# Group 0 of a recurrent-attention output moved inside SBUF, and its rows kept in a new order

## The chip, the core and the metric

One core of a Trainium2 chip runs the whole program. Its engines work side by side, each with its own queue of instructions: PE (TensorE, matrix products), DVE (VectorE), ACT (ScalarE), POOL (GpSimd) and SP (SyncE, which here only issues transfers). Sixteen DMA engines move data between DRAM and SBUF, and within SBUF. SBUF is the core's memory of 128 partitions; products land in PSUM, which has eight banks here called "bank". The metric is the device time of one execution in microseconds; less is better.

## The reference

Inputs q, k, v, alpha are (4, 8, 768, 48): batch, heads, sequence, head width. Weights w1, w2 are 384 x 1024, w3 is 1024 x 1024, w_out is 1024 x 384.

```python
for t in range(S):
    state = alpha[:, :, t, :, None] * state + np.einsum('bhd,bhe->bhde', k[:, :, t], v[:, :, t])
    y[:, :, t] = np.einsum('bhd,bhde->bhe', q[:, :, t], state)
x = y.transpose(0, 2, 1, 3).reshape(B * S, H * D)
a = x @ w1
b = x @ w2
return (a * b @ w3) @ w_out
```

So x has 3072 tokens of 384 values: head h fills the values 48 h to 48 h + 47.

## The kernel before

**Tiling.** The sequence is cut into 24 chunks of 128 tokens (`n`), 6 for each batch. Three chunks make a group (`g`, 384 tokens), so there are 8 groups. Two heads share the 128 partitions as a pair: head 2j in partitions 0 to 47, head 2j+1 in 64 to 111 (DP = 64); partitions 48 to 63 and 112 to 127 hold padding. There are four pairs (NP = 4).

**Attention.** The loop `for n in range(N + 1)` overlaps steps of neighbouring chunks. `load_a` and `load_kq` fetch alpha, k and q; `logs` and `decays` build decays with a logarithm, a product with a triangular matrix and two exponentials (L324, L343, L349, L350); `decayed(n + 2)` multiplies k and q with them on DVE (L359); `transposed` turns them with PE (L381) and ACT copies them out (L383); `scores` multiplies k and q (L454, later L430) and DVE masks the result (L457, later L440); `attend_state` and `attend` form the output y transposed, 48 or 64 rows of a head by 128 tokens, in two banks (L474, L485, later L482). Here the halves of the partitions mean something else: the lower half (0 to 63) carries heads 0 to 3, the upper half heads 4 to 7, 48 rows each and 16 rows of padding, and `y[i]` block `j` holds head 2j + i of each half.

**Output of attention.** ACT copies the two banks into a tile x (L489), `later` takes two transfers for it, and `store()` hands them to SP: 48 rows of each half go to the DRAM tile xd of the group (L305), whose rows are in the order of the reference, value 48 h + d.

**Gates.** `load_x(g)` brings xd[g] back as xT, 128 partitions by 3 blocks (`kk`) of 384 tokens: value kk x 128 + p (L501). For group 0 this stands at the end of chunk 4; for groups 1 to 4 at the top of chunks 8, 11, 15, 19, on SP; later visits to groups load on POOL. xT has one buffer. `split_x` cuts xT into three parts of fewer bits (L507, L508, L509), and for group 0 runs in chunk 6 (FIRST). `gate` multiplies them with w1 and w2, likewise in three parts (L515, 9 products in a run of three parts by three `kk`), and stores the product of both (L590).

**Weights.** w1 and w2 come as 64-bit floats and are turned into 32-bit floats by `to_fp32` (DMA L236; ACT L244, L249; DVE L245, L248, L251, L252, L253), and cut in three by `load_gates` (L260, L262, and L265 or two PE products L276, L277). A call handles 128 rows (one `kk`) by 512 columns (a `half`) of one weight: 12 calls, 6 for each half. Up to three are fetched ahead; half 0 is done in chunk 5, half 1 afterwards. `to_fp32` already takes several sources for w3 and w_out, each into its rows of the tile.

**Order.** The text's order, priorities of a planner, and `after_marks` (an instruction goes behind a named one on its engine) fix each engine's order. Waits are put in for every pair of accesses that touch the same bytes.

**After attention** the remaining gates run (`todo`, `visits`), w3 and w_out are multiplied into one matrix, and `project` forms the output.

Of the kernel before, what the change touches and what calls it, by code (L numbers as in the profile page):

```python
# [10 lines left out]
FP32 = mybir.dt.float32  # L11
# [37 lines left out]
def kernel(  # L49
# [12 lines left out]
    nc = tc.nc  # L62
    B, H, S, D = q.shape
    C = 128
# [5 lines left out]
    DP = 64  # L70
# [8 lines left out]
    LATE = 10  # L79
    PAIRED = 8  # L80
    TURNED = 8
    assert D <= DP and DM % C == 0 and DF % CW == 0 and S % C == 0 and N % G == 0
    assert DM <= 512 and TG <= 512

# [138 lines left out]
    for x in Ts + decs:  # L223
        nc.gpsimd.memset(x, 0.0)

    def to_fp32(*srcs, width=None):

        n = width or sum(src.shape[1] for src in srcs)
        raw = rawp.tile([C, n], I64, tag="raw", name="raw")
        for i, src in enumerate(srcs):  # L230
            if width:
                rows = ds(i * src.shape[0], src.shape[0])
                to = raw[rows] if len(src.shape) == 2 else raw[rows].rearrange("p (b c) -> p b c", b=src.shape[1])
            else:
                to = raw[:, ds(i * src.shape[1], src.shape[1])]
            nc.sync.dma_start(out=to, in_=src)  # L236
        yield
        words = raw.bitcast(U32).rearrange("p (n w) -> p n w", w=2)
        low, high = words[:, :, 0], words[:, :, 1]

        mant = cvt.tile([C, n], FP32, tag="mant", name="mant")
        top = mant.bitcast(U32)
        rest = cvt.tile([C, n], FP32, tag="rest", name="rest", bufs=2)
        nc.scalar.activation(rest, low, AF.Copy, scale=2.0 ** -52)  # L244
        nc.vector.tensor_scalar(top, high, 0x000FFFFF, 0x00100000, op0=ALU.bitwise_and, op1=ALU.bitwise_or)  # L245

        power = cvt.tile([C, n], U32, tag="power", name="power", bufs=2)
        nc.vector.tensor_scalar(power, high, 20, 0x7FF, op0=ALU.logical_shift_right, op1=ALU.bitwise_and)  # L248
        nc.scalar.activation(power, power, AF.Relu, scale=2.0 ** 23, bias=rebias)  # L249
        yield  # L250
        nc.vector.scalar_tensor_tensor(mant, top, 2.0 ** -20, rest, op0=ALU.mult, op1=ALU.add)  # L251
        nc.vector.scalar_tensor_tensor(power, high, 0x80000000, power, op0=ALU.bitwise_and, op1=ALU.bitwise_or)  # L252
        nc.vector.tensor_mul(mant, mant, power.bitcast(FP32))  # L253
        yield
        return mant

    def load_gates(i, kk, half):
        w = yield from to_fp32((moe_w1, moe_w2)[i][ds(kk * C, C), ds(half * CW, CW)])
        h, l, m = (w12[half][:, x, i, kk, :] for x in range(3))
        nc.scalar.activation(h, w, AF.Copy, scale=(1.0 - 2.0 ** -13) / P)  # L260
        yield
        mark["l"] = nc.vector.scalar_tensor_tensor(l, h.bitcast(FP32), -P, w, op0=ALU.mult, op1=ALU.add).ins  # L262
        done.append((i, kk, half))
        if half:
            nc.vector.scalar_tensor_tensor(m, h.bitcast(FP32), P + 1.0, w, op0=ALU.mult, op1=ALU.subtract)  # L265
        else:
            thirds.append((m, h, l))
# [33 lines left out]
    def store():  # L301

        while later:
            dst, src = later.popleft()
            nc.sync.dma_start(out=dst, in_=src)  # L305
# [171 lines left out]
    def attend(n):  # L477
        (y, heads), ms, vc = st.pop(("y", n)), st.pop(("ms", n)), st.pop(("v", n))
        for j, i, to in heads:
            if turned(n):  # L480
                w = vts[n % 2][:, j, :] if i else vc[:, 2 * j, :]
                nc.tensor.matmul(to[:, DP:], w, ms[:, i, j, DP:], start=False,  # L482
                                 stop=(j % HP == HP - 1), skip_group_check=True)
            else:
                nc.tensor.matmul(to, vc[:, 2 * j + i, :], ms[:, i, j, :], start=(n % NCH == 0 and j % HP == 0),  # L485
                                 stop=(j % HP == HP - 1), skip_group_check=True)
        x = work.tile([C, HP, 2, C], FP32, tag="x", name="x", bufs=4)
        for i in range(2):
            copied = nc.scalar.copy(x[:, :, i], y[i])  # L489
        ends_of_part1[1] = copied.ins  # L490
        x = x.rearrange("p j i t -> p (j i) t")

        g, c = divmod(n, G)
        to = xd[g].rearrange("(b h d) t -> b d h t", b=2, d=D)
        for half in range(2):
            later.append((to[half, :, :, ds(c * C, C)], x[ds(DP * half, D)]))


    def load_x(g, queue=nc.sync):
        st["xT", g] = xp.tile([C, KM, TG], FP32, tag="xT", name="xT")  # L500
        queue.dma_start(out=st["xT", g], in_=xd[g].rearrange("(k p) t -> p k t", p=C))  # L501

    def split_x(g, i):
        x = st.pop(("xT", g))
# [184 lines left out]
    for n in range(N + 1):  # L689
        if not 1 < n < FIRST:  # L690
            store()
        if n in loads:
            load_x(loads[n])
        if n != 1 and not 2 < n <= FIRST:
            load_a(n + 5)
        raws = (3, 3, 3, 3, 2, 2, 3, 3)[n] if n < 8 else 4
        for m in (n + 3,) * (n <= FIRST) + (n + 4,) * (n >= FIRST):
            load_kq(m)
            if 2 < n <= FIRST and m == n + 3:
                load_a(n + 5)  # L700
            if 1 < n < FIRST:
                store()
            if n < FIRST - 2:
                fetch(raws)
        if n >= FIRST:
            load_v(n + 2)
        if n:
            attend_state(n - 1)
        if n < N:
            scores(n)  # L710
        else:
            for j in range(NP):
                for i in range(2):
                    attend_low(n - 1, j % 2, i, i ^ (j < 2))
        transposed(n + 1)
        if n == 1:
            decays(3)
            load_a(6)
            with after_marks(("e", 3)):
                logs(4)  # L720
        if n == FIRST + 1:
            run(2)
        if n < FIRST:
            with after_marks("pool"):
                load_v(n + 2)
        if n - 2 in begin and n > FIRST:
            g, tiles = begin[n - 2]
            with after_marks(("ms", n), ("qkT", n + 1)):
                split_x(g, 0)
            fill.extend(gate(g, f) for f in tiles)  # L730
        if n == FIRST:
            with after_marks("l", ("qkT", n + 1)):
                split_x(0, 0)
            fill.extend(gate(0, f) for f in begin[n - 3][1])
        pieces = ((3, 3, 2, 0) if n > FIRST + 3 else (0, 3, 3, 0))[(n - FIRST) % 4] if n >= FIRST else 0
        if n == 0:
            with after_marks(("qkT", 0)):
                logs(2)
            decays(2)
            with after_marks(("e", 2)):  # L740
                logs(3)
        early, ready = n < FIRST, len(thirds) if n > 2 else n // 2
        marks = (*[("qkT", n + 1)] * (n < N - 1), *[("qk", n + 1), ("ms", n)] * early, *["x3"] * (n - 2 in begin and n > FIRST))
        if n < N - 2 and n != FIRST:
            with after_marks(*marks):
                convert(2 if early else 1, raws)
        advance(n)
        turn_v(n)
        if n:
            attend(n - 1)  # L750
        outer(n)
        if n > FIRST:
            third(ready)
        run(pieces > 0)
        if early:
            with after_marks(*marks):
                convert(1, raws)
        with after_marks(*[("ms", n)] * (n < 3)):
            decayed(n + 2)
        if not early:  # L760
            with after_marks(*[("qkT", n + 1)] * (n < N - 4)):
                logs(n + 4)
        if n == 4:
            load_x(0)
        convert(early and n > 0, raws)
        run(pieces > 1)
        if n:
            decays(n + 3)
        if n <= FIRST:
            third(ready)  # L770
        if 0 < n < FIRST:
            with after_marks(("e", n + 3)):
                logs(n + 4)
        if n == FIRST:
            with after_marks("x3", ("e", n + 3)):
                convert(2, raws)
        elif n < N - 2:
            convert(n == FIRST - 1 if early else n % 3 == 0, raws)
        if n == FIRST - 1:
            assert len(done) == 2 * KM  # L780
        run(pieces > 2)
        if n == N - 3:
            while begun:
                convert(1)
            weights.extend(load_out(j) for j in range(KF))
            fetch(4)
# [90 lines left out]
```

## Time and profile before

| | us |
|---|---|
| median of 3 runs | 464.25 |
| lowest and highest | 463.48, 465.31 |
| span of the profiled execution | 462.8 |
| PE busy in it | 446.9 |
| DVE busy | 371.7 |
| ACT busy | 276.4 |
| POOL busy | 95.1 |

The span runs from the first to the last instruction of one profiled execution; the timed runs add what lies around it. A line of a timeline gives start, length, engine, line of the kernel, operation, what is written <- what is read, and count; in square brackets stands how long the engine had been idle before it and what released it. The transfers, by the page's list of issues (KB each, median us from issue to landing):

```profile
raw<-in_moe_w_dram SPq DMA_DIRECT2D x12, 512.0 KB, 5.8
xT<-xd POOLq DMA_DIRECT2D x9, 576.0 KB, 4.7
kq<-in_q_dram SPq DMA_DIRECT2D x24, 192.0 KB, 5.4
xd<-x SPq DMA_DIRECT2D x48, 96.0 KB, 3.9
xT<-xd SPq DMA_DIRECT2D x5, 576.0 KB, 5.0
```

### The profile page before, as it was taken

How to read it: one execution, taken by the hardware profiler on the slowest of the kernel's cores; microseconds unless marked ns; L12 is line 12 of the kernel's file. 1: busy time of each engine (PE TensorE's matmuls, PEld its weight loads, DVE VectorE, ACT ScalarE, POOL GpSimd, SP SyncE). 2: the span in 40 equal slices, each digit the busy share in tenths (PEclk: the TensorE clock that was granted, in tenths of full speed). 3: DMA queues.
4: the chain of work that ended last, by engine and by line, in shares of the span. 5: the costliest groups of instructions: out<-in, count | busy, mean ns of one | idle time of the engine just before them, and what ended most of it. 6: DMA issues, size and time to landing. Idle time of an engine off the chain costs nothing.

```text
span 462.8 us, 11150 instructions
## 1 busy us (share of the span) xinstructions
PE 446.9 (97%) x4296; PEld 423.2 (91%) x4296; DVE 371.7 (80%) x610; ACT 276.4 (60%) x544; POOL 95.1 (21%) x186
## 2 busy tenths in 40 slices
PE   4998999999999999999999999999999999999996
PEld 2675699898999989999999999999999999999996
DVE  2779997999979988999998999997542967776671
ACT  4685975767658563988875676764545443333430
POOL 6234232325414430121221201212010000000000
PEclk9999999999999999999999999999999999999999
DMA  9999999999999974466856446412115875665511
GB/s 173 254 208 228 261 224 192 248 209 219 184 227 193 234 165 138 130 224 212 235 178 196 146 128 177 149 52 86 51 48 153 243 210 180 186 178 159 166 51 52
DMA packets 148869, 80.37 MB, mean 174 GB/s; under 512 B 97392, under 2 KB 138608, under 8 KB 148816
## 3 DMA queue, kind: packets, MB, share of 16 engines
q1 hardware_dynamic: 143040, 64.44, 57.3%
q0 software_dynamic: 5776, 15.22, 11.0%
q8 instruction: 34, 0.56, 0.5%
q14 instruction: 19, 0.16, 0.1%
HBM read 57.58 MB, written 22.06 MB: 172 GB/s over the span
## 4 chain that ended last, share of the span: by engine, by line
PE 88%; DVE 4%; DMA 4%; ACT 2%; issue 1%; SPq 0%; DVEq 0%; ACTq 0%
PE bank L515 72%; DMA kq<-in_q_dram 3%; PE bank L381 3%; PE bank L430 3%; PE bank L482 2%; PE bank L474 2%; PE bank L340 1%; PE bank L393 1%; PE bank L346 1%; PE bank L454 1%; PE bank L343 1%; PE bank L419 1%; DVE qk L359 1%; DVE ms L457 1%; PE bank L485 1%
## 5 line engine op out<-in xcount | busy, mean ns | idle before, releaser
L515 PE MATMUL bank<-x,w 128*128 128x384 f32 x1152 | 210.2, 337 | 1.7 <-ACT qkT L383 1.1
L515 PEld LDWEIGHTS bank<-x,w 128*128 128x128 f32 x1152 | 200.2, 188 | 4.1 <-ACT qkT L383 1.4
L515 PE MATMUL bank<-w3o,ab 128*128 128x384 f32 x576 | 100.2, 336 | 0.0
L515 PEld LDWEIGHTS bank<-w3o,ab 128*128 128x128 f32 x576 | 99.9, 188 | 0.0
L540 ACT ACTIVATE bank<-bank 128x384 f32<-128x384 f32 x96 | 45.6, 476 | 43.4 <-PE bank L515 43.1
L524 ACT ACTIVATE t<-bank 128x384 f32<-128x384 f32 x64 | 31.9, 499 | 54.9 <-PE bank L515 54.9
L590 POOL DMA_DIRECT2D abd<-ab x45 | 25.8, 573 | 137.9 <-DVE ab L576 121.3
L383 ACT COPY qkT<-bank 128x512 f32<-128x512 f32 x48 | 26.2, 596 | 24.8 <-PE bank L381 24.8
L641 DVE TENSOR_TENSOR ab<-abl,ab 128x1024 fp32r<-128x1024 f32 x24 | 29.3, 1223 | 12.3 <-ACT ab L640 12.3
L640 ACT ACTIVATE ab<-abl 128x1024 fp32r<-128x1024 f32 x24 | 25.5, 1061 | 20.2 <-PE bank L515 18.4
L515 PE MATMUL bank<-wo,w3T 128*128 128x384 f32 x192 | 35.9, 334 | 0.0
L576 DVE TENSOR_TENSOR ab<-bank,r 128x384 f32<-128x384 f32 x44 | 24.1, 548 | 12.5 <-PE bank L515 6.3
L515 PEld LDWEIGHTS bank<-wo,w3T 128*128 128x128 f32 x192 | 33.5, 188 | 0.0
L249 ACT ACTIVATE power<-power,rebias 128x512 uint32<-128x512 uint32 (+1 forms) x36 | 25.3, 701 | 12.6 <-DVE power L248 12.4
L359 DVE TENSOR_TENSOR qk<-kq,e 128x768 f32<-128x768 f32 x24 | 23.1, 964 | 11.3 <-ACT e L350 7.9
L526 DVE SCALAR_TENSOR_TENSOR o<-bank,t 128x384 f32<-128x384 f32 x24 | 13.4, 557 | 23.0 <-issue 13.7
L642 DVE SCALAR_TENSOR_TENSOR ab<-ab,abl 128x1024 fp32r<-128x1024 f32 x24 | 29.2, 1217 | 0.0
L526 DVE SCALAR_TENSOR_TENSOR r<-bank,t 128x384 f32<-128x384 f32 x40 | 22.0, 550 | 6.8 <-PE bank L515 3.4
L251 DVE SCALAR_TENSOR_TENSOR mant<-mant,rest 128x512 f32<-128x512 uint32 (+1 forms) x36 | 23.4, 649 | 3.7 <-ACT rest L244 3.7
L252 DVE SCALAR_TENSOR_TENSOR power<-raw,power 128x512 uint32<-128x512 uint32 (+1 forms) x36 | 23.5, 653 | 2.4 <-ACT power L249 2.4
L253 DVE TENSOR_TENSOR mant<-mant,power 128x512 f32<-128x512 f32 (+1 forms) x36 | 23.6, 655 | 0.5
L244 ACT ACTIVATE rest<-raw 128x512 f32<-128x512 uint32 (+1 forms) x36 | 23.3, 649 | 0.0
(102 smaller groups left out, 675.2 us busy)
## 6 DMA issues: line engine op xcount, KB each, us to landing
abl<-abd SPq DMA_DIRECT2D x24, 512.0 KB, 4.7
abd<-ab POOLq DMA_DIRECT2D x45, 192.0 KB, 3.2
raw<-in_moe_w_dram SPq DMA_DIRECT2D x64, 128.0 KB, 3.4
raw<-in_moe_w_dram SPq DMA_DIRECT2D x12, 512.0 KB, 5.8
xT<-xd POOLq DMA_DIRECT2D x9, 576.0 KB, 4.7
kq<-in_k_dram SPq DMA_DIRECT2D x24, 192.0 KB, 5.2
kq<-in_q_dram SPq DMA_DIRECT2D x24, 192.0 KB, 5.4
xd<-x SPq DMA_DIRECT2D x48, 96.0 KB, 3.9
```

The source lines that it names most:

```text
L249: nc.scalar.activation(power, power, AF.Relu, scale=2.0 ** 23, bias=rebias)
L359: mark["qk", n] = nc.vector.tensor_mul(qks[n % 3][:, :, :, 0:D], st.pop(("kq", n)), st.pop(("e", n)).rearrange("p i (h d) -> p i h d", h=H ...
L383: mark["qkT", n] = nc.scalar.copy(qkT[:, :, :, ds(DP * half, DP)], tp[half]).ins
L515: nc.tensor.matmul(p, w[part][i], x[part][i], start=start and part == parts[0] and i == 0, stop=stop and part == parts[-1] and i == n - 1, ...
L524: nc.scalar.activation(t, p1, AF.Copy, scale=(1.0 + 1.0 / P) * scale)
L526: nc.vector.scalar_tensor_tensor(to, p2, scale, t, op0=ALU.mult, op1=ALU.add)
L540: nc.scalar.activation(p, p, AF.Copy, scale=1.0 + 1.0 / P)
L576: nc.vector.tensor_mul(ab, p, r[0])
L590: (nc.gpsimd if late else nc.sync).dma_start(out=abd[g][:, f, :], in_=ab)
L640: nc.scalar.activation(t[:, 0], ab, AF.Copy, scale=1.0 - 2.0 ** -13)
L641: nc.vector.tensor_sub(t[:, 1], ab, t[:, 0].bitcast(FP32))
L642: nc.vector.scalar_tensor_tensor(t[:, 2], t[:, 0].bitcast(FP32), -1.0 - 1.0 / P, ab, op0=ALU.mult, op1=ALU.add)
```

## The change

For chunks 0 to 2 (group 0) the output of attention is no longer sent to DRAM and brought back. ACT copies it straight into xT: three of the four heads of each partition half lie there as the three blocks, and the fourth head (48 rows) goes into the tile x. Six transfers a chunk then move 16 rows each of that fourth head into the padding partitions (48 to 63 and 112 to 127) of the three blocks. So the order of the 384 values on partitions and blocks is another one, and the rows of w1 and w2 are loaded in that order, by four transfers of 48, 16, 48 and 16 rows in place of one of 128. The other groups keep their order in DRAM, and their load of xT takes four transfers in place of one. Group 0's x is written to DRAM from xT at chunk 7, in the order of xT, for the later visit.

```diff
+    SD = D // KM
...
+    def runs(kk):
+
+        return [(i * DM // 2 + start, size, i * DP + at) for i in range(2)
+                for start, size, at in ((D * kk, D, 0), (D * KM + SD * kk, SD, D))]
+
-    def to_fp32(*srcs, width=None):
+    def to_fp32(*srcs, width=None, at=None):
...
-                rows = ds(i * src.shape[0], src.shape[0])
+                rows = ds(at[i] if at else i * src.shape[0], src.shape[0])
...
     def load_gates(i, kk, half):
-        w = yield from to_fp32((moe_w1, moe_w2)[i][ds(kk * C, C), ds(half * CW, CW)])
+        src = (moe_w1, moe_w2)[i][:, ds(half * CW, CW)]
+        w = yield from to_fp32(*(src[ds(start, size)] for start, size, _ in runs(kk)), width=CW, at=[at for *_, at in runs(kk)])
...
         x = work.tile([C, HP, 2, C], FP32, tag="x", name="x", bufs=4)
+        if n < G:
+            if n == 0:
+                st["xT", 0] = xp.tile([C, KM, TG], FP32, tag="xT", name="xT")
+            to, part = st["xT", 0][:, :, ds(n * C, C)], x[:, HP - 1, 1]
+            nc.scalar.copy(part, y[1][:, HP - 1])
+            nc.scalar.copy(to[:, 0::2], y[0])
+            nc.scalar.copy(to[:, 1], y[1][:, 0])
+            for half in range(2):
+                for kk in range(KM):
+                    later.append((to[ds(half * DP + D, SD), kk], part[ds(half * DP + kk * SD, SD)]))
+            return
...
     def load_x(g, queue=nc.sync):
         st["xT", g] = xp.tile([C, KM, TG], FP32, tag="xT", name="xT")
-        queue.dma_start(out=st["xT", g], in_=xd[g].rearrange("(k p) t -> p k t", p=C))
+        if g == 0:
+            queue.dma_start(out=st["xT", g], in_=xd[g].rearrange("(p k) t -> p k t", k=KM))
+            return
+        for at in range(0, C, DP):
+            h = xd[g][ds(at // DP * DM // 2, DM // 2)]
+            queue.dma_start(out=st["xT", g][ds(at, D)], in_=h[0:KM * D].rearrange("(k p) t -> p k t", p=D))
+            queue.dma_start(out=st["xT", g][ds(at + D, SD)], in_=h[KM * D:].rearrange("(k p) t -> p k t", p=SD))
...
     for n in range(N + 1):
         if not 1 < n < FIRST:
             store()
+        if n == FIRST + 1:
+            nc.sync.dma_start(out=xd[0].rearrange("(p k) t -> p k t", k=KM), in_=x0)
...
         if n == FIRST:
+            x0 = st["xT", 0]
...
-        if n == 4:
-            load_x(0)
```

## The prediction

> **What bounds the kernel now.** I read the page first (engines, the DMA row), then the table of windows, the chain of waits, and then the timelines of DVE and SP for the stretch where the diff acts.
>
> ```profile
> span 462.8 us, 11150 instructions
> PE 446.9 (97%) x4296; PEld 423.2 (91%) x4296; DVE 371.7 (80%) x610; ACT 276.4 (60%) x544; POOL 95.1 (21%) x186
> DMA  9999999999999974466856446412115875665511
> ```
>
> TensorE leaves only 15.9 us of the span idle. The DMA row is full for the first 14 slices of 11.6 us, the attention stage. The windows show where the idle time is:
>
> ```profile
> 30.00:40.00 10.00, 8.73 (x141) 6.72 (x142) 7.57 (x14) 6.49 (x15) 2.80 (x4) 1.00 1.07 202
> 40.00:50.00 10.00, 8.72 (x122) 6.27 (x118) 9.08 (x17) 7.31 (x16) 4.62 (x7) 1.00 1.19 245
> 50.00:60.00 10.00, 9.66 (x119) 7.80 (x116) 9.46 (x16) 9.57 (x22) 2.39 (x4) 1.00 0.99 249
> 60.00:70.00 10.00, 10.00 (x134) 9.20 (x134) 9.97 (x19) 6.07 (x16) 3.61 (x7) 1.00 1.14 236
> ...
> 200.00:220.00 20.00, 20.00 (x115) 20.00 (x114) 19.96 (x39) 17.46 (x37) 4.17 (x8) 1.00 0.65 198
> ```
>
> Columns: stretch, length, then PE, PEld, DVE, ACT, POOL busy, clock, DMA share, GB/s. Before 60 us PE has gaps (2.9 us in 30 to 60); from 60 on it has about 2.2 us up to 180 and none from 180 to 440. Work before 60 us that comes earlier or later moves the end one for one; work after it hides under PE. So I ask what sets the pace from 27 to 57 us. The chain of waits there:
>
> ```profile
> 27.01 7.37 DMA kq<-in_q_dram
> ...
> 34.51 0.96 DVE qk L359
> 35.47 1.20 DVE ms L457 x2
> ...
> 39.74 7.11 DMA kq<-in_q_dram
> ...
> 46.97 0.96 DVE qk L359
> ```
>
> Two loads of q, and between them DVE. DVE's timeline says how long it really waited:
>
> ```profile
> 34.51 0.96 DVE L359 TENSOR_TENSOR qk<-kq,e 128x768 f32<-128x768 f32 x1 [2.36 <-DMA kq<-in_q_dram]
> ...
> 46.97 0.96 DVE L359 TENSOR_TENSOR qk<-kq,e 128x768 f32<-128x768 f32 x1 [0.22 <-DMA kq<-in_q_dram]
> ```
>
> Hence 2.36 us for the q of 27.01 and only 0.22 us for that of 39.74: after 34.5 us DVE is nearly always busy and the second q is just in time. The loads come from SP's queue, in order:
>
> ```profile
> 29.54 3.33 SPq L305 DMA_DIRECT2D xd<-x  x2
> 32.97 0.41 SPq L236 DMA_DIRECT2D raw<-in_moe_w_dram  x1
> ...
> 37.54 1.16 SPq L305 DMA_DIRECT2D xd<-x  x2
> 38.80 0.40 SPq L236 DMA_DIRECT2D raw<-in_moe_w_dram  x1
> 39.30 0.39 SPq L153 DMA_DIRECT2D kq<-in_k_dram  x1
> 39.74 2.56 SPq L154 DMA_DIRECT2D kq<-in_q_dram  x1
> ...
> 49.08 0.37 SPq L501 DMA_DIRECT2D xT<-xd  x1
> ```
>
> An issue with room in front of it takes about 0.40 us and 0.05 us to the next; the long ones (3.33, 2.56) are held back because the engines are full.
>
> **The change, part by part.**
>
> *Round trip of group 0.* Removed: six stores (L305) and the load at 49.08 with its 1.3 us wait for the stores. The split does not wait for that load: its first ACT instruction starts at 54.68, right behind the copies of qkT (53.74 for 1.10 us). So the latency saved is worth 0. What is saved is DMA time. Cost of a packet: over the run SP's queue has 143040 packets, 64.44 MB, 57.3% of 16 engines, so 29.7 ns for 450 B; between 40 and 58 us 11560 packets, 4.17 MB, 98.7%, so 24.6 ns for 361 B. A line through both gives 4 ns + 0.057 ns/B (estimate): 512 B 33 ns, 1536 B 92 ns, 4608 B 267 ns. A store of 192 packets of 512 B is 0.40 us, six are 2.4 us; the load of 384 packets of 1536 B is 2.2 us. Added are 18 moves of 16 rows of 512 B, 0.033 us each, 0.6 us. Net 4.0 us less for the engines between 29 and 54 us. Who gains? The q of 27.01 is ahead of the first store, so its 2.36 us stays. The q of 39.74 saves DVE 0.22 us. Value -0.2, bounds -2.6 (both waits vanish) and 0; I take -0.2, as the order of issue supports only that.
>
> *SP's issues.* From 29.54 to the end of the q issue at 47.68 (46.21 and 1.47) SP issues 16 transfers in 18.1 us. After the change the 6 stores are 18 moves and the 2 weight loads are 8: 34 issues, at 0.45 us 15.3 us. It fits, with 2.8 us left, in place of the 10.9 us now spent held back (18.1 less 16 x 0.45). Queued behind the moves and the weight quarters are the k and q of the next chunk; DVE (L359) and then the masks (L457) wait for them. In a chunk, q comes behind 4 + 3 issues more, 3.15 us if nothing absorbs them, less 0.8 us of engine time for two stores, 2.4 us. Bounds: 0 (the held-back time takes all) and +4.1 (none of it does: the first rival below). As the second q is just in time and the held-back time of 10.9 us is over three times the 3.15 us, I take +0.5.
>
> *ACT.* Each of chunks 0 to 2 has three copies for two. L489's 128x256 copy has a median of 377 ns, L383's 128x512 a mean of 596: 0.86 ns a column, so 128 columns 267 ns (estimate). 267 + 377 + 267 less 754 is 157 ns, 0.47 us in all. They free the banks that L381's weight loads waited for (1.1 us in the run). Bounds 0 and +0.5; taken +0.2, since ACT idles 6.5 us behind DVE in that stretch.
>
> *Store of x0 at chunk 7.* The same 576 KB in 128 rows of 4608 B: 128 x 267/16 = 2.1 us of engine time, near 64 us; cover: PE is full there. The load for group 1 (72.08) must now wait for it, as it reuses the tile: 64 + 0.4 + 3.9 to land (L305's median) + 2.1 is 70.4, before 72.08. If it is 2 us late, that load lands at 72.08 + 2 + 5.0, still before its split at 80.00. Taken 0, bounds 0 and +1.5.
>
> *Weights and x later.* Six more weight loads in quarters (18 issues) and the loads for groups 1 to 4 in four parts (12 issues) are 30 x 0.45 = 13.5 us of SP over some 100 us; its queue is held back there too. Behind each load of x stands a load of alpha, for which ACT (L324) waited 1.4 us once. Bounds 0 and +2 (that wait twice, a third of it covered); taken +0.2. On POOL nine loads at 0.75 us become 36 at 0.54 (its store L590) to 0.75 us: 1.4 to 2.3 us more each. Nearest case: issued 194.46, split at 202.60, 8.1 us; 0.75 + 4.7 to land leaves 2.7. Taken 0.
>
> Work of PE and DVE is the same. Sum: -0.2 + 0.5 + 0.2 + 0 + 0.2 = +0.7 us on the profiled 462.8 us. The median of the runs, 464.25, is 1.45 us more, which lies around the span; so **465.0 us**, no change to be told: 0.5% (2.3 us) is about what a measurement here can tell.
>
> A rule against the change: the Trainium skill, "DMA: Bandwidth & Descriptors", section "Rules for kernel authors", says to merge small transfers, since below 64 KB one pays mostly overhead, and its section "Anatomy of one DMA" (for transfers that GpSimd issues) puts the fixed part near 2.0 us. Six moves one after the other would by that be 12 us a chunk, from 44.5 to 56.5, 1.8 us after the split's 54.68; the sum would be +2.5. The trace speaks against a strict series: the stores' shortest time to landing is 1.9 us, yet two are issued within 1.16 us.
>
> **Rivals.**
>
> *SP becomes the bound (slower).* Place: chunks 2 to 5, 29.5 to 57 us. It decides once an issue costs over 18.1/34 = 0.53 us. Price: 18 more issues at 0.45, 8.1 us, less the 4.0 us of engine time, +4.1: 468.3. For it: 34 issues against 16, and q just in time. Against: the quick rows are 0.31 to 0.48 us, and 10.9 us of held-back time are there to absorb them.
>
> *Copies wait for moves (slower).* If chunk 1's copies into the tile of group 0 are ordered behind chunk 0's moves into it, ACT, due at 29.44, waits until 29.5 + 2.7 + 3.9 = 36.1: +6.7, 471.0 at least. Against: two chunks' stores go into neighbouring columns of one DRAM tile at 50.03 and 51.74 with no wait for a landing between.
>
> *DMA relief counts in full (faster).* Engines are full; if another order puts both q loads ahead, DVE's 2.36 + 0.22 go: 461.7. Against: nothing removed stands before 27.01, and DVE has no other wait over 0.7 us up to 57.
>
> *Nothing of the kind: the round trip was hidden.* This is my forecast.
>
> **How the numbers follow.** Forecast 0.50 (own range 463 to 466.5), SP bound 0.28, copies waiting 0.05, relief 0.17. So faster 0.17, same 0.50, slower 0.33. The range 461.4 to 469.8 holds the first, the second and most of the relief case.
>
> **What would show it.** SP's timeline at 29 to 48 us: 34 short issues, few above 1 us. DVE's L359 near 34.5 with about 2.4 us of wait, and near 47 with under 1 us. First gate matmul (L515, now 57.68) within 1 us of that. ACT copies without waits for DMA. I am wrong if L359 waits over 2 us in several chunks, if the first gate moves by over 2 us, or if the order of an engine's instructions in 20 to 60 us is another one.

## The result, and the profile after

The changed kernel takes **514.39 us** (median of 6 runs, 512.8 to 519.19) beside 464.53 us for the kernel before: ratio 1.1081, 95% interval 1.1048 to 1.1113. It is slower by 50 us where +0.7 was forecast; the range ended at 469.8. Times here and below are medians; one execution of the kernel whose weights are cut by 48 and 16 rows, 497.75 us, fell into a slower state and is left out of its 491.84 us (with it 493.04). The profiled execution has a span of 511.1 us. Lines of the changed kernel carry other numbers: L389 is the old L381 (turning qk on PE), L367 the old L359 (qk on DVE), L348 and L324 the old L340 and L316 (product and logarithm of the decays), L243 the old L236 (load of a weight piece), L313 the old L305, L540 the old L515 (gates); L251, L258, L259, L260 and L268 are the conversion of weights (old L244, L251, L252, L253, L260).

The page of the changed kernel, span, engines and granted clock:

```profile
span 511.1 us, 11324 instructions
PE 466.5 (91%) x4296; PEld 437.2 (86%) x4296; DVE 372.1 (73%) x610; ACT 280.7 (55%) x547; POOL 103.3 (20%) x210
PEclk9879789978978998999999999999999999999999
```

The span is 48.3 us longer. PE is busy 19.6 us longer with the same 4296 matmuls (466.5 less 446.9) and idle 28.7 us longer (44.6 against 15.9). The clock row (granted clock in tenths, by 40 slices) was 9 throughout before; now it drops in the first 16 slices. The windows show it together with PE's gaps (columns as before):

```profile
30.00:40.00 10.00, 10.00 (x108) 6.81 (x110) 4.32 (x9) 4.23 (x10) 3.92 (x8) 0.76 1.10 179
40.00:50.00 10.00, 7.87 (x118) 6.16 (x118) 7.01 (x13) 6.96 (x16) 3.96 (x7) 1.00 0.96 152
50.00:60.00 10.00, 7.58 (x86) 5.26 (x86) 5.32 (x10) 4.86 (x10) 1.99 (x3) 0.83 0.81 129
60.00:70.00 10.00, 6.25 (x68) 4.37 (x68) 5.04 (x10) 5.45 (x11) 1.98 (x3) 0.83 0.74 150
...
200.00:220.00 20.00, 19.95 (x390) 18.66 (x389) 15.44 (x28) 10.82 (x25) 6.46 (x14) 1.00 0.53 132
```

In 60 to 70 us PE does 68 matmuls; before, 134. DVE is busy 5.0 us there where it was 10.0, and the DMA engines have room (0.81 and 0.74 in 50 to 70 us, before 0.99 and 1.14). No engine is full there: they wait for each other. The first gate matmul, at 57.68 us before, is here:

```profile
79.86 3.39 PE L540 MATMUL bank<-x,w 128*128 128x384 f32 x18
```

So 22.2 of the 48.3 us are lost before it and 26 behind it: from 80 to 200 us PE is idle for 16.6 us, at a granted clock of 0.87 to 0.91, where it was idle for 2.2 us at 1.00.

The chain of waits, in the stretch where it held two loads of q before:

```profile
37.64 0.58 ACT rest L251
38.25 0.64 DVE mant L258
38.89 0.57 issue
39.73 0.68 DVE mant L260
40.41 0.88 DVE qk L367
41.42 0.72 PE bank L389 x16
```

The chain runs through the conversion of a weight piece (L251, L258, L260) and only then to qk, for which PE waits. In the whole run the table of waits has none of DVE's qk for a load of k or q (2.6 us in two waits before): in this order it is not late data that holds qk, but what stands ahead of it on DVE. PE's own waits in 8 to 100 us say the same (engine, what it wanted, what it waited for; us in total, times, longest):

```profile
PE bank L389 <- DVE qk L367: 15.4, 7, 4.2
PE bank L348 <- ACT x L324: 4.3, 1, 4.3
```

Before, the same two were 2.3 us in 2 waits and 0.3 us. And SP's queue in that stretch:

```profile
32.92 7.62 SPq L313 DMA_DIRECT2D xT<-x  x6
40.58 1.97 SPq L243 DMA_DIRECT2D raw<-in_moe_w_dram  x4
...
46.76 5.46 SPq L313 DMA_DIRECT2D xT<-x  x6
52.27 1.97 SPq L243 DMA_DIRECT2D raw<-in_moe_w_dram  x4
...
57.15 4.48 SPq L313 DMA_DIRECT2D xT<-x  x6
```

18 moves take 17.6 us of the queue, 0.98 us each and not the 0.45 of the forecast.

### The profile page after: what moved, and what is told of

It is laid out like the page before. It is cut to its first block, busy times and chain, and to the rows that moved or that the text cites. A ratio compares the mean times of both kernels' runs of the same rounds, so it can differ in the third digit from the quotient of the medians.

```text
span 511.1 us, 11324 instructions
## 1 busy us (share of the span) xinstructions
PE 466.5 (91%) x4296; PEld 437.2 (86%) x4296; DVE 372.1 (73%) x610; ACT 280.7 (55%) x547; POOL 103.3 (20%) x210
## 3 DMA queue, kind: packets, MB, share of 16 engines
q0 software_dynamic: 6160, 15.22, 10.9%
## 4 chain that ended last, share of the span: by engine, by line
PE 74%; DMA 6%; DVE 5%; ACT 4%; issue 2%; POOL 1%; SPq 1%; POOLq 0%; ACTq 0%; DVEq 0%
PE bank L540 62%; DMA dec<-ends 3%; DMA ends<-e 2%; PE bank L389 2%; PE bank L438 2%; PE bank L490 2%; PE bank L482 2%; PE bank L348 1%; PE bank L427 1%; ACT qkT L391 1%; ACT x L532 1%; DVE qk L367 1%; DVE x L533 1%; DVE mant L258 1%; DMA kq<-in_k_dram 1%
## 5 line engine op out<-in xcount | busy, mean ns | idle before, releaser
L540 PE MATMUL bank<-x,w 128*128 128x384 f32 x1152 | 212.2, 340 | 2.4 <-ACT x L532 1.7
L540 PEld LDWEIGHTS bank<-x,w 128*128 128x128 f32 x1152 | 202.2, 190 | 4.7 <-ACT x L532 1.8
L540 PE MATMUL bank<-w3o,ab 128*128 128x384 f32 x576 | 100.2, 336 | 0.0
L540 PEld LDWEIGHTS bank<-w3o,ab 128*128 128x128 f32 x576 | 99.9, 188 | 0.0
L615 POOL DMA_DIRECT2D abd<-ab x45 | 25.8, 574 | 126.3 <-DVE ab L601 106.5
L540 PE MATMUL bank<-wo,w3T 128*128 128x384 f32 x192 | 35.9, 334 | 0.0
L389 PE MATMUL bank<-ident,qk 64*128 64x64 f32 x384 | 19.9, 254 | 15.4 <-DVE qk L367 15.4
L540 PEld LDWEIGHTS bank<-wo,w3T 128*128 128x128 f32 x192 | 33.5, 188 | 0.0
L389 PEld LDWEIGHTS bank<-ident,qk 64*128 64x128 f32 x384 | 16.6, 162 | 19.2 <-issue 14.0
L551 DVE SCALAR_TENSOR_TENSOR r<-bank,t 128x384 f32<-128x384 f32 x40 | 21.8, 552 | 13.9 <-PE bank L540 10.3
L258 DVE SCALAR_TENSOR_TENSOR mant<-mant,rest 128x512 f32<-128x512 uint32 (+1 forms) x36 | 23.6, 655 | 9.9 <-ACT rest L251 9.6
L367 DVE TENSOR_TENSOR qk<-kq,e 128x768 f32<-128x768 f32 x24 | 22.8, 951 | 8.3 <-ACT e L358 8.3
L259 DVE SCALAR_TENSOR_TENSOR power<-raw,power 128x512 uint32<-128x512 uint32 (+1 forms) x36 | 23.5, 654 | 0.6 <-ACT power L256 0.6
```

Source lines behind the costliest of these rows:

```text
L367: mark["qk", n] = nc.vector.tensor_mul(qks[n % 3][:, :, :, 0:D], st.pop(("kq", n)), st.pop(("e", n)).rearrange("p i (h d) -> p i h d", h=H ...
L389: nc.tensor.transpose(tp[half][:, i, j, :], qk[s, i, 2 * j:2 * j + 2, :], ident[s, s])
L540: nc.tensor.matmul(p, w[part][i], x[part][i], start=start and part == parts[0] and i == 0, stop=stop and part == parts[-1] and i == n - 1, ...
L551: nc.vector.scalar_tensor_tensor(to, p2, scale, t, op0=ALU.mult, op1=ALU.add)
L615: (nc.gpsimd if late else nc.sync).dma_start(out=abd[g][:, f, :], in_=ab)
```

## The experiments

Each experiment had theories with a forecast of their own. **A**: a transfer to few, neighbouring partitions is slow in the DMA engines. **B**: the small moves hold up SP's queue. **C**: the number of transfers on SP costs the time. **D**: the planner, given other transfers, puts the instructions of all engines into another order, and that order is slow. **E**: load_a waits for POOL's read of a row of alpha, which costs the time behind the first gate matmul. **T** stands for A to C together, the transfers whatever the order. "Before" is timed beside each kernel (464.1 to 464.8 us).

### One part undone or done alone, in the order that the planner then makes

**Whole weight pieces in the changed kernel:**

```diff
-        w = yield from to_fp32(*(src[ds(start, size)] for start, size, _ in runs(kk)), width=CW, at=...)
+        w = yield from to_fp32(src[ds(kk * C, C)])
```

> The changed kernel with each piece of w1 and w2 loaded by one transfer of 128 rows again, in the old order of rows (so the gates multiply x by other rows of the weights; shapes and amounts are the same). Theory A, the quarters of 48 and 16 rows hold the DMA engines about twice as long as one transfer of 128 rows (3.1 us against 1.5 us a piece in the two traces): most of the 50 us goes, 464 to 480 us, first gate product before 65 us. Theory B, the eighteen small moves drain SP's queue and the loads of k and q behind them come late: 500 us or more, because the moves are all still there. Theory C, the number of issues on SP: 485 to 505, since half of the added issues go.

Measured: 479.25 us, ratio 1.031 (1.0265 to 1.0355); first gate matmul at 60.75 us, as theory A had it. 35 of the 50 us go with the cut of the weights.

**The cut alone, in the kernel before,** in rows and in columns:

```diff
+        cut = ((0, 48), (48, 16), (64, 48), (112, 16))
+        w = yield from to_fp32(*(src[ds(start, size)] for start, size in cut), width=CW, at=[start for start, _ in cut])
```

> The kernel before with only this added: each piece of w1 and w2 comes by four transfers of 48, 16, 48 and 16 rows into the same rows of the tile, in the natural order. Theory A: 490 to 515 us, the bulk of the loss from this edit alone. Theory B: under 472 us. Theory C: 475 to 495.

Measured: 491.84 us, 1.0585 (1.0528 to 1.0641), first gate 80.6 us: the cut by itself makes most of the loss.

```diff
+        w = yield from to_fp32(*(src[:, ds(c * C, C)] for c in range(CW // C)))
```

> The kernel before with each piece of w1 and w2 cut in four by columns: four transfers of 128 rows by 128 columns (1 KB a row) in place of one. As many issues and bytes as with 48, 16, 48 and 16 rows, but each transfer reaches all 128 partitions. Theory A (the few partitions of a transfer cost): 462 to 472 us. Theory C (the number of issues costs): as slow as the cut by rows, within 5 us of it. Theory B: under 472.

Measured: 471.15 us, 1.0159 (1.0105 to 1.0213). As many transfers cost 6.5 us here and 27.2 us there, so their number alone (theory C) is not the cause. That spoke for A, but this kernel's order of instructions also stayed near the old one (on DVE it is the same up to 34 us), and that of the cut by rows did not (on DVE another one from 15.6 us on).

**The changed kernel without its 18 moves** (the fourth pair of group 0 is then not written), **and with x of the later groups loaded whole:**

```diff
-                    later.append((to[ds(half * DP + D, SD), kk], part[ds(half * DP + kk * SD, SD)]))
+                    pass
```

> The changed kernel without the eighteen moves inside SBUF (the fourth head of group 0 is left out of x, the padding rows stay as they are). Theory A: 495 us or more, at most some 15 us less than the changed kernel. Theory B: 464 to 480. Theory C: 500 to 510, as a sixth of the added issues go.

Measured: 508.82 us, 1.0949 (1.09 to 1.0999); only 5.6 us go, and theory B, which had 464 to 480 us, fails in this order.

```diff
-        for at in range(0, C, DP):
...
+        queue.dma_start(out=st["xT", g], in_=xd[g].rearrange("(k p) t -> p k t", p=C))
```

> The changed kernel with x of groups 1 to 7 (and the later visit of group 0) loaded by one transfer of 128 partitions again, in the old order (so these gates multiply x by weight rows of the other order). Theory A, the same cause in the four transfers of x: 5 to 12 us of the 50 go, 502 to 509. Theory E, the loss after the first gate comes from alpha, which waits for POOL's copy of a row out of the buffer: under 3 us go, 511 to 516.

Measured: 495.17 us, 1.0631 (1.0574 to 1.0689). 19.2 us go, more than either theory had; E's 511 to 516 us is out. The first gate matmul stays at 80.07 us, so all of it was lost behind that point.

With both edits, whole weights and whole x:

> The changed kernel with both the weights (w1, w2) and x of the groups loaded by single transfers of 128 partitions, in the old order; left of the change are the copies into the split's input, the eighteen moves and the store of group 0 (the gates multiply other rows). Theory A: all that is left are the moves, 466 to 474 us. Theory E: near the 479 of the kernel with whole weights, 476 to 482.

Measured: 475.2 us, 1.0216 (1.0173 to 1.026), just outside both ranges. x in four is worth 19 us beside cut weights and 4 us beside whole ones (479.25 less 475.2): the parts do not add up, which no fixed price per transfer explains.

### Same order, other partitions

The kernel before with each piece in four transfers of 32 rows, once neighbouring, once every fourth row; the planner gives both the same order on every engine:

```diff
+        w = yield from to_fp32(*(src[ds(r * Q, Q)] for r in range(C // Q)), width=CW)
...
+        w = yield from to_fp32(*(src[r::4] for r in range(4)), width=CW, step=4)
```

> The kernel before with each piece of w1 and w2 cut into four transfers of 32 neighbouring rows (partitions 0 to 31, 32 to 63 and so on). Theory A (few neighbouring partitions share few ways into SBUF, so such a transfer is slow): between the cut by columns (471) and the cut by 48, 16, 48 and 16 rows (493): 478 to 490, mean packet of 4096 B near 250 ns. Theory C (four issues cost what they cost): 471, as the cut by columns.

> The same four transfers of 32 rows with the same instructions in the same order on every engine, but transfer r takes partitions r, r + 4, r + 8 and so on up to r + 124, so each reaches the whole width of SBUF. Theory A: 465 to 473 us, packet of 4096 B near 200 ns. Theory D, the planner put the engines' instructions into another order and that order is slow: the same time as with neighbouring rows, within 3 us, since the order is the same. Theory C: the same too.

Measured: 492.67 us, 1.0601 (1.0544 to 1.0659), outside what A and C had, and 490.9 us, 1.0547 (1.0505 to 1.0589), as D had it. In the records of the first 30 us a packet of 4096 bytes takes 288 ns with neighbouring rows and 236 ns with spread ones (200 before), yet the time hardly moves. A is not the cause of most of it. What the two share with the 48/16 cut is the order of instructions, which in the traces is the same in all three on DVE, ACT, POOL and SP.

### The transfers and the order taken apart

Here every engine is held to a given order: each instruction gets an edge to the one that stands before it in that order, for issue only, without a wait.

```diff
+    for name, order in ORDER.items():
+        traced = [i for i in nc.cur_bb.bb.instructions if i.engine == getattr(mybir.EngineType, name)]
+        turn = [traced[at + k] for at, count in order for k in range(count)]
+        for one, two in zip(turn, turn[1:]):
+            tc.add_manual_dep(two, one.name, mybir.DependencyInfo(mybir.DependencyClass.NoSync, mybir.DependencyReason.DATA), reason="order")
```

> The kernel before, with each weight piece still moved by one transfer of 128 rows, but every engine (and SP's queue) is held to the order of instructions that the planner made when the pieces were cut into 4 transfers of 32 rows (that kernel took 492.7 us). Theory D (the order that the planner makes from its own view of the cut transfers is what costs the time): 485 to 495 us, first gate matmul at 75 us or later, although no transfer is cut. Theory T (the cut transfers themselves land late, the order is harmless): 464 to 468 us. A part of each: about 478 us.

Measured: **491.54 us**, 1.0612 (1.0565 to 1.0659), first gate 76.0 us.

> The kernel with each weight piece cut into 4 transfers of 32 rows (492.7 us), but every engine and SP's queue held to the order of the kernel before, the four quarters at the place of the one whole piece. Theory D (order): 464 to 470 us, with the weights' 4096-byte packets still near 290 ns. Theory T (transfers): 488 to 495 us. If both orders give the transfers' price a part, 475 to 480 us.

Measured: **476.58 us**, 1.0265 (1.0229 to 1.0301), first gate 64.4 us; packets of 4096 bytes at 298 ns in the first 30 us.

| | order of before | order of the 32-row cut |
|---|---|---|
| whole pieces | 464.3 | 491.5 |
| pieces cut by rows | 476.6 | 492.7 |

The order alone costs 27.3 us with not one transfer changed; the cut transfers alone cost 12.3 us; together 28: in the slow order the cut adds only 1.1 us. That the slow order leaves the transfers time would explain it; no run shows it. D holds, and T has a smaller share. Two rivals fall. SP issues its transfers in the order of before up to 143 us in the kernel with whole pieces, and DVE's qk never waits for a load there, so the loss up to there lies in the order on DVE, ACT, POOL and PE and not in SP's. And holding an order shows no cost of its own: the changed kernel held to the old one, with whole transfers and without moves, takes 463.82 us (below).

What is slow in that order can be read from the kernel with whole pieces. Its ACT and PE:

```profile
24.27 0.72 ACT L249 ACTIVATE power<-power,rebias 128x512 uint32<-128x512 uint32 x1
26.61 0.63 ACT L260 ACTIVATE w<-mant 128x512 fp32r<-128x512 f32 x1 [1.63 <-DVE mant L253]
27.15 0.83 ACT L316 ACTIVATE x<-x 128x768 f32<-128x768 f32 x1
```

```profile
23.18 0.62 PE L393 MATMUL bank<-v,qk 128*64 128x48 f32 x16
28.03 2.93 PE L340 MATMUL bank<-x 128*128 128x384 f32 x4 [4.23 <-ACT x L316]
```

and the same two instructions in the kernel before:

```profile
22.03 0.85 ACT L316 ACTIVATE x<-x 128x768 f32<-128x768 f32 x1
```

```profile
22.94 1.56 PE L340 MATMUL bank<-x 128*128 128x384 f32 x4 [0.27 <-ACT x L316]
```

The logarithm L316 that PE needs stands ahead of a piece's conversion in the old order and behind it in the new one, behind L260, which waits 1.63 us for DVE. It runs at 27.15 instead of 22.03, and PE stands still for 4.23 us. On DVE the same happens to qk (L359), which runs at 26.50 behind the conversion's L253 and ran at 22.56 ahead of L251. The windows of the slow kernel then show the second price:

```profile
24.00:28.00 4.00, 0.00 (x0) 0.00 (x0) 3.04 (x5) 2.35 (x4) 0.00 (x0) 0.74 1.30 207
28.00:30.00 2.00, 1.97 (x3) 1.17 (x4) 0.00 (x0) 0.00 (x0) 1.76 (x4) 0.50 0.98 236
30.00:32.00 2.00, 2.00 (x20) 0.78 (x18) 0.00 (x0) 0.87 (x2) 0.79 (x3) 0.50 1.06 201
```

After the gap PE's clock is 0.50, so L340's four matmuls take 2.93 us for 1.56, and DVE's masks wait for PE in turn. PE's waits in 8 to 100 us, first in this kernel, then with cut pieces in the old order (there L382 is L381, L360 is L359):

```profile
PE bank L381 <- DVE qk L359: 13.9, 6, 4.2
PE bank L340 <- ACT x L316: 4.2, 1, 4.2
```

```profile
PE bank L382 <- DVE qk L360: 3.7, 3, 2.0
```

The 13.9 and 4.2 us are near the 15.4 and 4.3 us of the changed kernel, without its transfers; on DVE the two orders are the same up to 60 us. With the old order 3.7 us of the first are left (2.3 in the kernel before) and 0.4 us of the second, though the transfers are cut. Of the 27.3 us, 18.3 are lost before the first gate matmul; the 9 behind it were not followed.

### The changed kernel in the old order

The edits are those above (whole weights, whole x, no moves) with the list of the old order; what the change adds stands directly behind what it replaces.

> The changed kernel (514.4 us) with every engine and SP's queue held to the order of the kernel before; what the change adds stands directly behind what it replaces (four quarters in the place of a whole piece, six moves in the place of two stores, the third copy behind the two, the store of x0 where chunk 7 begins). All its transfers stay as they are. Theory D (the planner's new order is most of the change's loss): 476 to 484 us, that is the 476.6 us that cut weights cost in the old order, and up to 7 more for the moves and x in four. Theory T (the transfers cost it, in any order): 500 us or more.

Measured: 495.99 us, 1.0689 (1.0642 to 1.0736): between the two theories.

> The same held order, and the weight pieces by one transfer of 128 rows each, rows as before (group 0 is then multiplied with weights whose rows stand in another order). Left of the change: copies into xT, 18 moves, x of the later groups in four transfers, store of x0. Planner's own order for this kernel gave 479.25 us. Theory D: 465 to 470 us. If the moves and the quarters of x themselves cost time: 475 us or more.

Measured: 484.09 us, 1.0416 (1.0385 to 1.0448).

> As the run above, and x of the later groups by one transfer of 128 partitions each, in the old order of rows (these groups too are then multiplied with other rows than the reference's). Left: copies into xT, 18 moves, store of x0, and no round trip of group 0's x, all in the order of the kernel before. Planner's own order gave 475.2 us. Theory D: 463 to 467 us, which also gives the price of the idea itself without cut weights: below 463 it would be a gain, above 468 the moves cost.

Measured: 471.82 us, 1.0151 (1.0123 to 1.018). The 12.3 us between the last two could be the price of x in four, but POOL and ACT of the former show a fault of the held order:

```profile
182.57 0.62 POOL L525 DMA_DIRECT2D xT<-xd  x1 [3.27 <-DVE mant L252]
201.35 0.62 POOL L615 DMA_DIRECT2D abd<-ab  x1 [16.59 <-DVE ab L588]
201.97 0.53 POOL L526 DMA_DIRECT2D xT<-xd  x1
```

```profile
207.44 1.16 ACT L532 ACTIVATE x<-xT 128x1152 fp32r<-128x1152 f32 x1 [7.12 <-DMA xT<-xd]
```

One quarter of that x went out at 182.57; the other three had been put behind a store (L615) that waits 16.59 us for DVE. So in two more kernels the four quarters stand together.

> The whole changed kernel held to the order of the kernel before, as in the earlier run of that kind (496.0 us), but the four quarters of each later x stand together at the place of the one load they replace. There, three of the four quarters of one late group stood behind a store of ab that waited 16.59 us on POOL, and the split waited 7.12 us for them. If that place was the price of x in four: 482 to 487 us. If four transfers of x cost it wherever they stand: 494 us or more. The distance to the 514.4 us of the planner's order is then what the order costs.

> As the run above with whole weight pieces (group 0 is multiplied with weights whose rows stand in another order); the earlier run of that kind took 484.1 us, and with whole x too 471.8 us. If the place of the three quarters was the price: 471 to 474 us. If x in four transfers costs time wherever it stands: 480 us or more.

Measured: **486.35 us**, 1.0473 (1.0449 to 1.0496), and 475.26 us, 1.0235 (1.0206 to 1.0265). 9 to 10 us of the earlier pair were the place of three transfers in a queue; the price of x in four, standing well, is 475.3 less 471.8, about 3.4 us, so 475.26 is a little above the 471 to 474 us expected. (The 475.3 us run also sends one pair of loads of k and q behind four moves and not ahead of them, so the 3.4 us hold only as far as that is free.)

> Whole weight pieces, whole x for the later groups, every engine held to the order of the kernel before, and without the 18 moves (the fourth pair of heads of group 0 stays where it was copied, so part of group 0's x is not written). Left of the change: the copies straight into xT, no round trip of group 0's x, and its store to memory at chunk 7. With the moves this took 471.8 us. If the moves on SP's queue are what cost the 7.4 us over before (theory B): 463 to 466 us. If the copies into xT and the store cost it: 469 to 472 us. A gain from the saved round trip would show as less than 462 us.

Measured: **463.82 us**, 0.9986 (0.997 to 1.0002): without the moves the rest of the idea shows no cost, and a gain of 0.3% at most. Theory B holds for the moves, 8.0 us in an unchanged order on DVE and POOL. SP's queue with the moves in it (471.8 us):

```profile
28.99 5.99 SPq L313 DMA_DIRECT2D xT<-x  x6
35.07 0.53 SPq L243 DMA_DIRECT2D raw<-in_moe_w_dram  x1
...
40.06 5.33 SPq L313 DMA_DIRECT2D xT<-x  x6
45.49 0.53 SPq L243 DMA_DIRECT2D raw<-in_moe_w_dram  x1
```

Where two stores took 3.33 and 1.16 us before, six moves take 5.99 and 5.33 us, and the next weight piece leaves at 45.49 instead of 38.80. Of the 18 moves, 14 take 0.53 to 0.66 us each and some 0.05 us to the next, in stretches where the DMA engines are full (mean share 0.94 in 40 to 45.4 us) and where they are not (0.61 in 52.6 to 56.8 us); the other four are held back, up to 2.82 us. The q behind that weight piece is issued at 46.55 instead of 39.74, and DVE waits for it 2.55 us where it waited 0.22:

```profile
51.33 0.96 DVE L367 TENSOR_TENSOR qk<-kq,e 128x768 f32<-128x768 f32 x1 [2.55 <-DMA kq<-in_q_dram]
```

So in the old order the transfers cost time by the way the first rival named, late loads of q. DVE's waits for q over the whole run, first with the moves alone (471.8 us), then with the moves, x in four and the weight pieces in four (486.4 us):

```profile
DVE qk L367 <- DMA kq<-in_q_dram: 5.8, 3, 2.7
```

```profile
DVE qk L367 <- DMA kq<-in_q_dram: 17.3, 6, 6.1
```

Without moves they are 1.9 us (463.8 us), with whole weight pieces 6.5 us (475.3 us): 10.8 us more for weight pieces in four, where the time grows by 11.1. In the planner's order the table has none of these waits.

### What the cut transfers cost by themselves

Both kernels of before with cut pieces, held to the old order:

> Each weight piece in 4 transfers of 32 rows that go to partitions r, r+4, r+8 and so on, with every engine held to the order of the kernel before (neighbouring partitions in the same order: 476.6 us, packets of 4096 bytes at a mean of 298 ns). Theory A (a transfer to neighbouring partitions alone is slow in the DMA engines): packets near 200 to 240 ns and 465 to 469 us. Theory C (four issues and four completions cost it, whatever the partitions): 474 to 478 us.

> Each weight piece in 4 transfers of 128 rows by 128 columns (packets of 1024 bytes), held to the order of the kernel before; the planner's own order for it gave 471.15 us. Theory A: all partitions are reached by each transfer, 465 to 469 us. Theory C: as with 4 transfers of rows, 474 to 478 us. If the planner's order was the 6.5 us: 465 us or less.

Measured: 473.74 us, 1.0194 (1.0172 to 1.0215), and 471.18 us, 1.0146 (1.0126 to 1.0167). Packets of 4096 bytes in the first 30 us: 219 ns spread against 298 ns neighbouring. Both times lie between what A and C expected, nearer to C. Of the 12.3 us some 3 are reach (476.6 against 473.7) and about 7 stay in the cheapest form, by columns (which also has four times as many packets, of a quarter the size); the 2.5 us between spread rows and columns have no cause shown. Columns take the same time in the planner's own order (471.15), so there the order cost nothing.

No version beats the kernel before beyond the noise. Theory E had no run of its own; its two forecasts, on x loaded whole, both missed.

## Why the prediction was wrong

The 50 us in steps, each from two runs. The sizes hold for this sequence: on top of the slow order a cut costs 1.1 us and not 12.3, and x in four costs 19 us in the planner's order beside cut weights and 3.4 in the old order beside whole ones.

| step | us | forecast |
|---|---|---|
| round trip gone, three copies, store of x0 (463.8, before 464.1) | -0.3 | 0.0 |
| 18 moves on SP (471.8 - 463.8) | +8.0 | in +0.5 |
| x of the later groups in four (475.3 - 471.8) | +3.4 | in +0.2 |
| weight pieces in four (486.4 - 475.3) | +11.1 | in +0.5 and +0.2 |
| the planner's order (514.4 - 486.4) | +28.0 | not priced |

*Round trip, ACT and store of x0* came out right in sum: -0.2, +0.2 and 0 were forecast, -0.3 was measured for the three together, with an interval of -1.4 to +0.1 us; the single terms were not measured. The rival "relief counts in full" falls: the 4.0 us less of engine time, were it there, moved the end by 0.3.

*The order* is the step that failed most. The sum took every engine's order as given ("Work of PE and DVE is the same") and priced each edit in place; another order as a loss stood only in the last sentence, as a sign of being wrong, with no chance and no price (the relief rival took one as a gain). So a term was put at nothing without a reason. It costs 27.3 us with whole pieces and 28.0 us in the changed kernel; these are two different new orders, alike on DVE only up to 60 us, so the equal size is no law. Why the planner puts conversions ahead for row cuts and not for column cuts was not shown.

*SP's issues* failed in two terms. A move was priced at 0.45 us of the queue and takes 0.94 (the 16.8 us of all 18 in the 471.8 us run); the median move takes 0.59 where the median store takes 0.44. And the 10.9 us of held-back time did not absorb the added issues: the stretch of 18.1 us, to the end of the third issue of q, became 23.6 us (28.99 to 52.56) though four moves went out behind it. The rival "SP becomes the bound" named this, with its point of decision at 0.53 us, and in the old order its mechanism is seen: q comes late and DVE waits. Its 4.1 us were half of the 8.0, and it had a chance of 0.28. In the changed kernel itself the slow order stands before it. And a quarter of a weight piece was priced as an issue alone, with the same work for the DMA engines; a packet of 4096 bytes takes the engines 306 ns in the changed kernel and 207 before, over the whole run. The Trainium skill, "DMA: Bandwidth & Descriptors", section "Rules for kernel authors", had been set aside in the forecast; in direction it was the better guide here, 8.0 us for 18 moves of 8 KB. But the split was not late by moves in series, as the forecast had worked it out: in the 471.8 us run it starts at 59.05 right behind the copies of qkT, and waits for no move.

*Weights and x later*: +0.2 with an upper bound of 2; x in four alone is +3.4, and 19 us in the planner's order beside cut weights, all behind the first gate matmul. The premise that work after 60 us hides under PE fails with it: PE's idle time from 80 to 200 us grew from 2.2 to 16.6 us. The share of this term in the weights' 11.1 was not separated from that of the first five chunks.

*What would show it* named the right places. 34 short issues did not appear, the first gate moved by 22 us and not by 1, and the order of instructions is another one, two of the three signs of being wrong. The third, long waits of L367 for q, is absent in the planner's order and appears in the old one (17.3 us in six waits). *Copies wait for moves* is not seen: in the table of waits ACT's copies into xT wait for no landing.

## What to carry to other kernels

Where a planner orders the instructions, a change to a transfer is a change to every engine's order: compare the orders of the two kernels before pricing anything, and hold the order in an experiment to see what the transfers themselves cost. A held order needs reading too, since three transfers in the wrong place cost 9 us here. A transfer cut in four is not four cheap issues: it cost 7 to 12 us on 12 pieces, and 18 moves of 8 KB cost more than the round trip that they replaced. Work that now hides under a full engine need not hide after the change: PE was nearly always busy from 60 us on before, and ran dry again between 80 and 200 us.

## What the runs showed of the hardware

**The clock after a gap.** In the kernel with whole pieces in the new order, a gap of 4.23 us in PE's work was followed by 4 us at clock 0.50; behind one of 2.13 us a little earlier L381 took 0.72 us, as before, and the window of 20 to 24 us reads 1.00. The Trainium skill, "TensorE: Matmul & The Clock Gate", section "Part 1: The HAM clock gate", says that an idle window of about 3.4 us halves the clock; the trace agrees. In the changed kernel, whose mean granted clock is 0.957 beside 1.000, 19.6 us of the 48.3 are PE being busy longer with the same matmuls.

**Reach of a transfer.** In the same order and number of transfers, neighbouring rows give 298 ns a packet of 4096 bytes and rows spread over all partitions 219 in the first 30 us (258 and 218 over the whole run; whole pieces 207). The traffic of the first 60 us, neighbouring rows first, then spread, which moves 6% more:

```profile
DMA packets 33963, 11.93 MB, mean 199 GB/s; under 512 B 31079, under 2 KB 32930, under 8 KB 33956
```

```profile
DMA packets 35038, 12.70 MB, mean 212 GB/s; under 512 B 31590, under 2 KB 33894, under 8 KB 35030
```

The Trainium skill, "SBUF — State Buffer", section "Door 1: The DMA port swizzle", says that bandwidth goes by how many of 16 ports the partitions reach, 8 for partitions 0 to 31. The packets agree; the end moved by 3 us only.
